# One tile and one transfer for both forms of v, and a new static order, in a one-core attention and mixture-of-experts kernel

## The chip, the core and the metric

The program runs on one core of a Trainium2 chip. The metric is the device time of one execution in microseconds (us). The core's engines work side by side, each through its own fixed list of instructions: TensorE (PE; PEld is its weight load), VectorE (DVE), ScalarE (ACT), GpSimd (POOL) and SyncE (SP), which here only issues transfers (DMAs). An instruction waits only for what it depends on and for what stands ahead of it on its engine.

## What is computed

Three stages over 4 batches of 8 heads, 576 tokens and 64 columns a head, all in float32:

```python
# attention: pooled form plus local form
v_d = v.reshape(B, H, 144, 4, D).mean(axis=3)              # q_d, k_d in the same way
out_up = np.repeat(sm_attn(q_d, k_d, v_d), 4, axis=2)      # 144 pooled queries, 144 pooled keys
mask = np.abs(pos[:, None] - pos[None, :]) < 4             # local: the 7 keys around a query
attn_out = out_up + softmax(where(mask, q @ k.T / 8, -1e9)) @ v
# gate stage on x: 2304 x 512
h = x @ w_in                                               # 2304 x 2048
g = (a0 + a1*h + a2*h**2 + a3*h**3) / (1 + |b0|*|h| + |b1|*h**2 + 1e-6)
x = g @ w_out
# soft routing to 8 experts of 4 slots each, two matrix products per expert, and back to the tokens
logits = x @ phi;  out = softmax_rows(logits) @ experts(softmax_columns(logits).T @ x)
```

## The kernel before

**Attention.** Two heads make a pair; there are 16 pairs, four to a batch. A pair lives in one set of four SBUF tiles (class `Set`, all tiles are called `at`). The first four pairs, 0 to 3, use four different sets, all others use set A. A pair needs `qk` (one transfer, `load_qk`) and v in two forms (`load_v`): `vd` for the pooled form, 80 rows by 1024 floats, and `vw`, 128 rows by 1280 floats, the local windows. For v these are two transfers, 320 and 640 KB. `pool_v` adds the four tokens of a group, in place, with two instructions (72x512 and 72x256). The pooled scores go through `scores_d` (PE `scd`), a maximum and a softmax; `turn_d` turns the 144 pooled keys in two halves of 72 onto partitions (PE `tpd`), `copy_d` copies each half out of PSUM on ACT (72x288), and `av_d` multiplies (PE `avd`, L650) before the local products `av` (L643). Sums go into `x`, which is split in a high and a low part, XH and XL.

**Weights.** Each of 8 blocks of `w_in` and `w_out` arrives as 1 MB of 8-byte words, and DVE narrows it to float32 in three steps (`nar`, `wst`, `wo`; L756, L761, L765). W is split in a high part (a cast) and a low part (a subtraction).

**Gate stage.** One step is 512 tokens by 256 columns: 24 products (PE `hps`, L889, 128x512), then a chain over ACT, DVE and POOL (`activate`: ab, cr, v, a, t, p, ln, ex, e, n, g), then transposes (`gt`), copies and logits (`lg`). Two PSUM pairs take turns: step m uses pair m % 2, and step m + 2 cannot write it until step m's chain has read it for the last time (its `e` or `n`, L990 and L993). The step with number 2, the third, is the first that waits for a pair in this way. The first two steps need all four first pairs of heads; pairs 0, 1, 3, 2 reach `avd` in that order.

**Order.** Nothing is scheduled on the chip. Class `Plan` collects all operations; the table `PLACE` gives each its place in one global order, the table `F` the engine where there is a choice (a ACT, d DVE, p POOL). Each engine gets its instructions in that order. The planner's durations (`PARTS`) and its `simulated` decide two more things: which DMA is held back until an earlier one has landed, and where `fillers` (products on zeros, `lg<-zero`, L1159 and L1162) stand in PE's list, at places where the planner foresees an idle PE.

**End.** The 32 transfers of expert weights (`we`, 1 MB each) run from 322 us on, most of them after 385 us.

Of the kernel before, what the change touches and what calls it, by code (L numbers as in the profile page):

```python
# [24 lines left out]
VROWS = 128  # L25
# [6 lines left out]
    pq="dppppppppdpppppp",  # L32
    pk="pddppppppppppppp",
    pv="pppppppppdpdpppp",
    nl="ppppppppddddppdp",
    nd="pppppppppdppdppd",
    wih="aaaaaaad",
    wil="pppppppd",
    xh="aaaaaaaadadadadda",
    xl="ppppdpdddpppddddd",  # L40
    cr="spppspppppppssppaappdpppppssspappsppa",
    t="dpdpddddddddddddddddpdddddddddddddddd",
    sd="rsssssrrssrsssrs",
    v="pppppppppppppppppdppdppppppppppppdppp",
    a="aaaaaadaaadaaaaaaaaaaaaaadaaaddaaadaa",
    g="ddfdfffddddddddddddddffddddddddddddff",
    gc="aaaaaaaaaadddaaaaadaaaaadadadadaaaaaadadadaadaaaaaaaaaadaadaaaadaaaaadaa",
# [3 lines left out]
    dm=(8,),  # L51
    ldqk=(4, 7, 31, 5, 125, 252, 361, 452, 546, 592, 716, 795, 822, 941, 1027, 1069),
    ldc=(6, 0),
    ldv=(42, 76, 163, 72, 219, 413, 466, 551, 602, 722, 800, 862, 944, 1063, 1092, 1176),
    coef=(1,),
    roots=(2,),
    rooted=(3,),
    pq=(9, 25, 58, 22, 149, 285, 412, 465, 580, 638, 726, 806, 842, 942, 1031, 1117),
    pk=(10, 21, 81, 16, 174, 335, 383, 453, 554, 617, 748, 796, 858, 960, 1033, 1134),
    sc=(17, 24, 44, 27, 236, 331, 437, 510, 585, 634, 744, 816, 895, 972, 1040, 1116),  # L60
    mx0=(18, 29, 52, 38, 250, 347, 440, 521, 590, 657, 746, 821, 901, 977, 1051, 1122),
    ms0=(19, 35, 53, 40, 265, 353, 446, 523, 593, 658, 756, 824, 910, 983, 1054, 1132),
    ex0=(23, 39, 56, 49, 266, 356, 463, 524, 594, 659, 757, 832, 911, 984, 1055, 1133),
    nl=(36, 43, 64, 71, 283, 394, 473, 536, 603, 685, 758, 841, 920, 996, 1067, 1142),
    nlp=(41, 69, 115, 103, 290, 404, 494, 549, 627, 717, 762, 843, 925, 1005, 1068, 1156),
    scd=(11, 55, 97, 26, 226, 336, 432, 504, 586, 695, 772, 812, 888, 981, 1077, 1141),
    mxd=(12, 61, 111, 30, 243, 341, 433, 506, 601, 704, 773, 815, 894, 982, 1085, 1145),
    msd=(13, 70, 116, 33, 263, 350, 451, 512, 616, 706, 777, 819, 897, 986, 1087, 1146),
    exd=(14, 78, 119, 37, 267, 352, 454, 515, 623, 707, 782, 829, 898, 993, 1091, 1152),
    nd=(28, 92, 124, 51, 273, 360, 461, 526, 674, 711, 783, 833, 915, 1035, 1109, 1155),  # L70
    ndp=(45, 99, 137, 84, 274, 391, 475, 535, 687, 725, 787, 840, 922, 1036, 1118, 1157),
    pv=(48, 126, 180, 87, 329, 430, 517, 567, 684, 754, 828, 878, 947, 1073, 1128, 1177),
    tp0=(54, 138, 144, 148, 295, 428, 501, 568, 633, 735, 793, 859, 937, 1022, 1113, 1169),
    cp0=(59, 140, 146, 156, 298, 431, 502, 574, 639, 753, 805, 873, 940, 1041, 1119, 1172),
    tp1=(67, 82, 166, 123, 325, 416, 505, 550, 631, 727, 814, 869, 969, 1023, 1094, 1161),
    cp1=(68, 83, 168, 129, 328, 417, 508, 555, 632, 728, 817, 876, 973, 1039, 1112, 1162),
    td0=(65, 127, 158, 104, 280, 398, 487, 558, 691, 740, 790, 853, 964, 1065, 1124, 1165),
    cd0=(66, 139, 159, 106, 293, 401, 491, 564, 698, 741, 802, 856, 976, 1078, 1125, 1170),
    td1=(47, 130, 142, 107, 275, 392, 482, 556, 690, 765, 811, 861, 935, 1076, 1126, 1163),
    cd1=(50, 136, 143, 108, 287, 393, 488, 561, 697, 766, 813, 867, 939, 1080, 1130, 1164),  # L80
    avd=(75, 141, 182, 162, 372, 460, 520, 569, 699, 775, 831, 881, 1001, 1081, 1131, 1178),
    av=(79, 151, 185, 170, 377, 464, 528, 578, 701, 776, 835, 883, 1002, 1084, 1138, 1179),
    od=(85, 152, 186, 171, 378, 474, 530, 579, 705, 785, 845, 884, 1015, 1086, 1140, 1181),
    x20=(86, 153, 195, 175, 390, 479, 539, 582, 719, 791, 854, 886, 1019, 1100, 1144, 1186),
    x21=(94, 155, 194, 172, 386, 478, 537, 583, 708, 794, 850, 885, 1016, 1099, 1143, 1184),
    x8=(91, 157, 193, 181, 384, 483, 531, 584, 720, 792, 851, 889, 1021, 1102, 1154, 1193),
    xh=(100, 173, 199, 176, 457, 516, 540, 589, 721, 799, 865, 887, 1057, 1108, 1150, 1187, 1300),
    xl=(101, 188, 208, 190, 472, 534, 577, 591, 739, 838, 871, 907, 1088, 1136, 1151, 1188, 1305),
    ldi=(15, 57, 93, 117, 145, 192, 169, 201),
    w0=(32, 60, 77, 110, 132, 135, 160, 167, 203, 196, 206, 183, 211, 209, 268, 278, 309, 311, 359, 355, 406, 408,  # L90
        448, 462, 541, 544),
    w1=(34, 62, 90, 112, 133, 150, 161, 178, 204, 198, 207, 187, 217, 227, 269, 279, 313, 318, 362, 357, 407, 409,
        449, 469, 542, 547),
    w2=(46, 63, 109, 118, 134, 165, 164, 179, 205, 200, 214, 191, 225, 230, 276, 281, 314, 319, 363, 369, 414, 420,
        455, 470, 545, 548),
# [1486 lines left out]
```

## Time and profile before

| | us |
|---|---|
| three runs | 489.97, 492.66, 494.0 (median 492.66) |
| the profiled execution | 491.29 |
| its span, from the first to the last instruction | 489.4 |
| PE busy | 458.5 (94%) |
| DVE busy | 401.6 (82%) |
| ACT busy | 321.1 (66%) |
| POOL busy | 246.8 (50%) |

Busy shares are means over stages. The opening (0 to 70 us) loads and narrows all gate weights and runs the first four pairs; the middle (70 to 380 us) is the gate stage with the other pairs between its steps; the rest are the last block, routing and experts. "Idle before" in a row is how long the engine stood still ahead of the instruction, and what ended that.

### The profile page before, as it was taken

How to read it: one execution, taken by the hardware profiler on the slowest of the kernel's cores; microseconds unless marked ns; L12 is line 12 of the kernel's file. 1: busy time of each engine (PE TensorE's matmuls, PEld its weight loads, DVE VectorE, ACT ScalarE, POOL GpSimd, SP SyncE). 2: the span in 40 equal slices, each digit the busy share in tenths (PEclk: the TensorE clock that was granted, in tenths of full speed). 3: DMA queues.
4: the chain of work that ended last, by engine and by line, in shares of the span. 5: the costliest groups of instructions: out<-in, count | busy, mean ns of one | idle time of the engine just before them, and what ended most of it. 6: DMA issues, size and time to landing. Idle time of an engine off the chain costs nothing.

```text
span 489.4 us, 12949 instructions
## 1 busy us (share of the span) xinstructions
PE 458.5 (94%) x5417; PEld 334.3 (68%) x5417; DVE 401.6 (82%) x568; ACT 321.1 (66%) x682; POOL 246.8 (50%) x231
## 2 busy tenths in 40 slices
PE   8687989999999999999999999999999989799995
PEld 5455766787687778766777676777766886343574
DVE  5799999999899899958898799899899988825233
ACT  3765586988767778866879776666867676610222
POOL 6588777864964557477174656624241514101000
PEclk9889999999999999999999999999999999999997
DMA  8999734566645102312402312380000399999966
GB/s 327 321 362 365 248 117 148 178 211 206 194 121 175 50 27 70 117 55 78 130 1 77 105 60 68 131 321 17 0 1 0 122 389 356 395 425 427 426 258 259
DMA packets 17866, 89.81 MB, mean 184 GB/s; under 512 B 2064, under 2 KB 2576, under 8 KB 11152
## 3 DMA queue, kind: packets, MB, share of 16 engines
q1 hardware_dynamic: 17808, 88.98, 50.4%
q8 instruction: 43, 0.70, 0.6%
q14 instruction: 15, 0.12, 0.1%
HBM read 80.06 MB, written 8.91 MB: 182 GB/s over the span
## 4 chain that ended last, share of the span: by engine, by line
PE 44%; DVE 20%; POOL 13%; ACT 11%; DMA 6%; issue 4%; SPq 0%; DVEq 0%; POOLq 0%; ACTq 0%
PE hps L889 16%; POOL gate L971 7%; DMA at<-in_qk 4%; PE op L1451 3%; DVE gate L990 3%; PE gt L1018 3%; ACT hps L989 3%; PE hps L907 2%; POOL gate L967 2%; DMA wst<-in_w_in 2%; PE av L643 2%; ACT gate L988 2%; PE hp L1330 2%; PE tpd L632 2%; PE scd L590 2%
## 5 line engine op out<-in xcount | busy, mean ns | idle before, releaser
L889 PE MATMUL hps<-XH,W 128*128 128x512 f32 x512 | 169.3, 400 | 1.6 <-DVE wst L765 1.0
L889 PEld LDWEIGHTS hps<-XH,W 128*128 128x128 f32 x512 | 96.6, 189 | 27.9 <-issue 2.5
L971 POOL TENSOR_TENSOR gate<-gate 128x1024 f32<-128x1024 f32 (+1 forms) x34 | 81.1, 2385 | 47.2 <-ACT gate L965 21.9
L889 PE MATMUL hps<-XL,W 128*128 128x512 f32 x256 | 100.4, 392 | 0.0
L967 POOL TENSOR_SCALAR gate<-gate,cf_sb 128x1024 f32<-128x1024 f32 (+1 forms) x25 | 32.1, 1284 | 72.3 <-ACT gate L975 70.1
L988 ACT ACTIVATE gate<-gate,one 128x1024 f32<-128x1024 f32 (+1 forms) x37 | 42.0, 1135 | 33.1 <-POOL gate L971 32.1
L990 DVE SCALAR_TENSOR_TENSOR gate<-gate,hps 128x1024 f32<-128x1024 f32 (+1 forms) x37 | 44.0, 1189 | 13.6 <-ACT hps L989 13.0
L889 PEld LDWEIGHTS hps<-XL,W 128*128 128x128 f32 x256 | 48.4, 189 | 9.1 <-POOL XL L734 0.2
L989 ACT ACTIVATE hps<-gate 128x1024 f32<-128x1024 f32 (+1 forms) x37 | 37.2, 1006 | 8.9 <-DVE gate L987 4.1
L729 ACT COPY G<-gt 128x512 f32<-128x512 f32 x56 | 32.6, 590 | 9.7 <-PE gt L1018 9.4
L564 POOL TENSOR_TENSOR at<-at 128x144 f32<-128x144 f32 x56 | 35.1, 627 | 4.4
L975 ACT ACTIVATE gate<-hps 128x1024 f32<-128x1024 f32 (+1 forms) x29 | 29.0, 999 | 5.4 <-PE hps L889 4.2
L971 DVE TENSOR_TENSOR gate<-gate,hps 128x1024 f32<-128x1024 f32 x24 | 29.2, 1216 | 3.9 <-ACT gate L965 3.8
L1018 PE MATMUL gt<-cf_sb,gate 128*128 128x128 f32 x192 | 28.7, 278 | 2.5 <-ACT G L729 1.1
L1018 PEld LDWEIGHTS gt<-cf_sb,gate 128*128 128x128 f32 x192 | 21.7, 141 | 11.3 <-ACT G L729 3.9
L602 ACT ACTIVATE at<-sc,at 128x38 f32<-128x38 f32 x144 | 28.2, 316 | 0.6
L987 DVE SCALAR_TENSOR_TENSOR gate<-gate,cf_sb,hps 128x1024 f32<-128x1024 f32 x22 | 28.1, 1277 | 0.6
L617 POOL TENSOR_TENSOR at<-at 128x432 f32<-128x432 f32 (+1 forms) x24 | 20.2, 849 | 12.6 <-DVE at L613 9.3
L994 DVE SCALAR_TENSOR_TENSOR gate<-gate 128x1024 f32<-128x1024 f32 x20 | 26.0, 1301 | 0.4
L907 PE MATMUL hps<-xs,W 128*128 128x256 f32 x192 | 24.3, 285 | 1.3 <-DVE A L993 1.2
L965 ACT ACTIVATE gate<-hps,cf_sb 128x1024 f32<-128x1024 f32 x19 | 22.9, 1208 | 3.9 <-PE gt L1018 2.6
L993 DVE SCALAR_TENSOR_TENSOR gate<-gate,cf_sb,hps 128x1024 f32<-128x1024 f32 x20 | 25.5, 1273 | 0.0
(182 smaller groups left out, 981.8 us busy)
## 6 DMA issues: line engine op xcount, KB each, us to landing
we<-in_w SPq DMA_DIRECT2D x32, 1024.0 KB, 10.1
at<-in_vw SPq DMA_DIRECT2D x16, 640.0 KB, 6.0
at<-in_qk SPq DMA_DIRECT2D x16, 579.0 KB, 5.5
wst<-in_w_in SPq DMA_DIRECT2D x8, 1024.0 KB, 8.7
wst<-in_w_out SPq DMA_DIRECT2D x8, 1024.0 KB, 6.0
at<-in_vd SPq DMA_DIRECT2D x16, 320.0 KB, 6.3
out<-late SPq DMA_DIRECT2D x17, 256.0 KB, 2.4
wo_dram<-wo SPq DMA_DIRECT2D x8, 512.0 KB, 7.9
```

The source lines that it names most:

```text
L564: nc.gpsimd.tensor_tensor(out=dst, in0=dst, in1=x[:, :, j], op=ALU.add)
L602: nc.scalar.activation(out=dst[:, i, :], in_=st["s", j][:, i, :], func=ACTF.Exp, scale=scale, bias=mx[:, i:i + 1], accum_out=None if sums ...
L729: nc.scalar.copy(out=out, in_=x)
L889: nc.tensor.matmul(hps[m][:, c].rearrange("p u t -> p (u t)"), lhsT=W[p][:, w, kk, 128 * c:128 * c + 128], rhs=x[xx][:, kk, :], start=(kk ...
L907: nc.tensor.matmul(out[:, c, :], lhsT=W[p][:, w, kk, 128 * c:128 * c + 128], rhs=xs[i][:, xx, kk, :], start=(kk == 0 and j == 0), stop=(kk ...
L967: (nc.vector if who == "d" else nc.gpsimd).tensor_scalar(out=out, in0=x, scalar1=coef[:, w:w + 1], scalar2=coef[:, b:b + 1], op0=ALU.mult, ...
L971: turned_over((nc.vector if who == "d" else nc.gpsimd).tensor_tensor(out=out, in0=x, in1=y, op=op), who)
L975: do("ab", "B", "H", lambda B, H: act(out=B, in_=H, func=ACTF.Abs, scale=coef[:, 4:5] if s2 else 1.0))
L988: do("ln", "C", "B", lambda C, B: act(out=C, in_=B, func=ACTF.Ln, bias=one))
L989: do("ex", "H", "C", lambda H, C: act(out=H, in_=C, func=ACTF.Exp, scale=-1.0))
L990: do("e", "B", "H", lambda B, H: stt(out=B, in0=B, scalar=1.0 + 1e-6, in1=H, op0=ALU.add, op1=ALU.mult))
L1018: nc.tensor.transpose(gt[n][:, u, 128 * c:128 * c + 128], g_of(n, c)[:, 128 * u:128 * u + 128], idn)
```

## The change

**Layout.** `v` is one array of 128 rows by 1792 floats: 1280 for the windows as before, and two areas of 256 for pooled keys 0 to 111 of either head (112 rows). Keys 112 to 143 of both heads lie in the last 256 of the window's columns, on rows 64 to 127, which the windows leave unused. One transfer of 896 KB takes the place of 320 and 640 KB, so 64 KB fewer for each pair, and 16 transfers fewer. Tiles are cut anew: V alone in the fourth tile, the turned scores and the gate's spare buffer in the second.

**Pooling v.** Three instructions take the place of two: 128x384, 128x128, 64x64. `pool_v` no longer overwrites v, but the next transfer of v waits for both the pooling and `av`; before, `vd` waited for the pooling and `vw` for `av`.

**Products.** Keys are turned as 112 and 32. Copying the 32 takes two ACT copies of 32x144 (one to each head's partitions), the 112 one of 112x288. `av_d` still has four products. Areas that must be zero are set once at the start by 8 more POOL memsets.

**Order and engines.** `PLACE` is new throughout, and `F` partly: the high part of the last W block goes from DVE to ACT. The planner's loads and fetch waits are costed differently. PE's list has 33 wide and 22 narrow fillers where it had 25 and 7; in each, six or seven wide ones open the program, and 6 wide ones stand in the last third.

```diff
-            self.qk, pdt, vds = cut(tags[0], 2 * S + 2 * PAD, 576, 256)
+            self.qk, pdr, half = cut(tags[0], 2 * S + 2 * PAD, 288, 384)
...
-            self.Vd, self.spare = cut(tags[3], 1024, 1024)
+            self.V, vds = cut(tags[3], 1792, 192)
...
     def load_v(s, bb, p):
-        begin(out=s.Vdl, in_=vd[bb, p])
-        begin(out=s.V[0:VROWS], in_=vw[bb, p])
+        begin(out=s.V, in_=v[bb, p])
...
-            turned_over(eng.tensor_tensor(out=x, in0=x, in1=y, op=ALU.add), who)
-            eng.tensor_tensor(out=dst, in0=x[:, 0:256], in1=x[:, 256:512], op=ALU.add)
+            turned_over(eng.tensor_tensor(out=s.half, in0=s.Vd[:, :, 0:128], in1=s.Vd[:, :, 128:256], op=ALU.add), who)
+            for r, b in ((slice(0, 128), slice(1, 3)), (slice(64, 128), slice(0, 1))):
+                eng.tensor_tensor(out=s.VdS[r, b], in0=s.half[r, b, 0:64], in1=s.half[r, b, 64:128], op=ALU.add)
...
+            for h in range(2):
+                x = st["t", 4][0:32, 64 * h:64 * h + 1]
+                nc.scalar.copy(out=s.PdR[64 + 32 * h:96 + 32 * h, h].rearrange("p (i q) -> p i q", i=3),
+                               in_=bass.AP(tensor=x.tensor, offset=x.offset, ap=[list(x.ap[0]), [136, 3], [1, 48]]))
...
+                nc.tensor.matmul(o, lhsT=s.VdS[0:LONG, 1 + h, :], rhs=s.PdT[0:LONG, h, :], start=True, stop=False)
+                nc.tensor.matmul(o, lhsT=s.VdS[:, 0, :], rhs=s.PdR[:, h, :], start=False, stop=True)
...
-        do("pv", "pv", pool_v, who["pv"], w="v VdS", pick=("pv", index))
+        do("pv", "pv", pool_v, who["pv"], r="v", w="VdS", pick=("pv", index))
...
-    wih="aaaaaaad",
+    wih="aaaaaaaa",
...
-    ldqk=(4, 7, 31, 5, 125, 252, 361, 452, 546, 592, 716, 795, 822, 941, 1027, 1069),
-    ldv=(42, 76, 163, 72, 219, 413, 466, 551, 602, 722, 800, 862, 944, 1063, 1092, 1176),
+    ldqk=(0, 11, 47, 6, 96, 275, 362, 452, 543, 575, 672, 795, 839, 919, 991, 1063),
+    ldv=(40, 58, 134, 80, 205, 408, 492, 547, 673, 716, 810, 867, 958, 1049, 1082, 1152),
```

On SP, the start of the program. Before (`at` is a set's tile, `wst` a raw weight block, `cf_sb` and `cb_sb` constants):

```order
L427 DMA cf_sb<-in_cf 128x390
L427 DMA at<-in_qk 128x1158 x2
L427 DMA cb_sb<-in_cb 128x470
L427 DMA at<-in_qk 128x1158
L427 DMA wst<-in_w_in 128x2048
L427 DMA wst<-in_w_out 128x2048
L427 DMA at<-in_qk 128x1158
L427 DMA at<-in_vd 80x1024
L427 DMA at<-in_vw 128x1280
```

Of the change:

```order
L421 DMA at<-in_qk 128x1158
L421 DMA cf_sb<-in_cf 128x390
L421 DMA at<-in_qk 128x1158
L421 DMA cb_sb<-in_cb 128x470
L421 DMA wst<-in_w_in 128x2048
L421 DMA at<-in_qk 128x1158
L421 DMA wst<-in_w_out 128x2048
L421 DMA at<-in_v 128x1792
```

The first weight block moved ahead of the third `qk`, and the fourth `qk` out of this stretch (it stands two transfers further on).

On DVE, the first weight blocks among the first pairs. Before (`at<-scd` and `at<-sc` are maxima of pooled and local scores; the second row of maxima here is that of pair 1's pooled scores):

```order
L595 TENSOR_REDUCE at<-sc 128x9
L756 TENSOR_SCALAR nar<-wst 128x1024
L595 TENSOR_REDUCE at<-scd 128x3
L761 SCALAR_TENSOR_TENSOR nar<-wst,nar 128x1024
L765 SCALAR_TENSOR_TENSOR wo<-wst,nar 128x1024
```

Of the change (L670 are pair 0's three sums after `av`):

```order
L759 TENSOR_SCALAR nar<-wst 128x1024
L589 TENSOR_REDUCE at<-sc 128x9
L606 TENSOR_REDUCE at<-at 128x9
L607 RECIPROCAL at<-at 128x9
L764 SCALAR_TENSOR_TENSOR nar<-wst,nar 128x1024
L768 SCALAR_TENSOR_TENSOR wo<-wst,nar 128x1024
L759 TENSOR_SCALAR nar<-wst 128x1024
L670 TENSOR_TENSOR at<-avd,at 128x4x64
L670 TENSOR_TENSOR at<-av,at 128x4x64
L670 TENSOR_TENSOR X_85<-av,at 128x64
L589 TENSOR_REDUCE at<-scd 128x3
```

The maximum of pair 1's pooled scores moved behind the whole `w_out` block and pair 0's sums.

On PE, what stands between the 24 products of a gate step and pair 7's pooled product `avd`, with the last of the 24 as the first row (`av` of the pair before stands right ahead of the 24, in both). Before:

```order
L889 MATMUL hps<-XH,W_983 128x512
L623 MATMUL tp<-cf_sb,at 38x128
L1018 MATMUL gt<-cf_sb,A_1087 128x128 x4
L632 MATMUL tpd<-cf_sb,at 72x128 x3
L842 MATMUL wq<-cf_sb,pp 128x32 x2
L632 MATMUL tpd<-cf_sb,at 72x128 x3
L823 MATMUL wt<-cf_sb,wo 128x128 x8
L623 MATMUL tp<-cf_sb,at 102x128 x4
L650 MATMUL avd<-at 64x144 x4
```

Of the change:

```order
L892 MATMUL hps<-XH,W_999 128x512
L617 MATMUL tp<-cf_sb,at 38x128
L627 MATMUL tpd<-cf_sb,at 112x128 x3
L629 MATMUL tpd<-cf_sb,at 32x128 x3
L845 MATMUL wq<-cf_sb,pp 128x32 x2
L617 MATMUL tp<-cf_sb,at 102x128 x4
L826 MATMUL wt<-cf_sb,wo 128x128 x4
L653 MATMUL avd<-at 64x144
```

Four transposes `gt` and four `wt` moved out of the stretch between the two products.

## Rows read from the trace of the kernel before

**Rows 1.** By stretch: length, then busy us (instructions) per engine, PEclk, DMA share, GB/s

```profile
0.00:12.50 12.50, 10.16 (x191) 6.93 (x194) 6.94 (x24) 4.69 (x17) 7.87 (x28) 1.00 0.86 328
12.50:20.00 7.50, 4.28 (x152) 3.37 (x152) 7.03 (x13) 5.06 (x27) 3.32 (x5) 0.78 1.02 346
...
22.40:70.60 48.20, 41.46 (x567) 29.59 (x567) 45.94 (x69) 30.44 (x62) 38.44 (x31) 0.93 0.77 266
70.60:380.00 309.40, 303.26 (x3456) 227.81 (x3455) 278.17 (x355) 234.38 (x489) 176.30 (x154) 1.00 0.32 104
380.00:440.00 60.00, 54.06 (x450) 38.87 (x450) 44.51 (x55) 33.94 (x58) 16.76 (x11) 1.00 0.87 341
440.00:489.40 49.40, 43.31 (x606) 26.59 (x598) 18.94 (x58) 10.36 (x20) 1.85 (x1) 0.95 0.84 343
```

**Rows 2.** Chain that ended last, 30 to 75 us: start, length, what

```profile
34.04 9.99 DMA wst<-in_w_in
...
44.12 0.71 DVE nar L756
...
69.43 1.19 DVE gate L993
```

**Rows 3.** Timeline of DVE and PE, 17 to 71 us: start, length, what, idle before

```profile
18.41 0.52 DVE L595 TENSOR_REDUCE at<-sc 128x9 f32<-128x342 f32 x1 [0.33 <-PE sc L580]
...
22.37 0.61 DVE L595 TENSOR_REDUCE at<-scd 128x3 f32<-128x432 f32 x1 [2.31 <-PE scd L590]
...
27.71 0.74 DVE L560 TENSOR_REDUCE at<-at 128x144 f32<-128x576 f32 x1
...
66.28 0.71 DVE L731 CAST W<-wst 128x1024 fp32r<-128x1024 f32 x1
...
69.34 1.27 DVE L993 SCALAR_TENSOR_TENSOR gate<-gate,cf_sb,hps 128x1024 f32<-128x1024 f32 x1
...
66.68 2.42 PE L1159 MATMUL lg<-zero 128*96 128x256 f32 x10
...
70.67 0.50 PE L889 MATMUL hps<-XH,W 128*128 128x512 f32 x1
```

**Rows 4.** Packets, rate, share of 16 engines: 42:44, 444:446 and 302.5:308 us

```profile
DMA packets 108, 0.47 MB, mean 235 GB/s; under 512 B 12, under 2 KB 12, under 8 KB 105
...
q1 hardware_dynamic: 108, 0.47, 103.4%
...
DMA packets 114, 0.84 MB, mean 422 GB/s; under 512 B 11, under 2 KB 11, under 8 KB 11
...
DMA packets 241, 1.00 MB, mean 182 GB/s; under 512 B 32, under 2 KB 32, under 8 KB 240
...
q1 hardware_dynamic: 240, 0.98, 54.1%
```

**Rows 5.** One steady hand-over: window transfer of v, landing, next product

```profile
136.08 0.33 SPq L427 DMA_DIRECT2D at<-in_vw  x1
...
at<-in_vw SPq DMA_DIRECT2D x1, 640.0 KB, 5.4
...
143.41 1.07 PE L823 MATMUL wt<-cf_sb,wo 128*128 128x128 f32 x8
...
144.84 0.72 PE L650 MATMUL avd<-at 72*64 72x144 f32 x8
145.49 0.66 PE L1018 MATMUL gt<-cf_sb,A 128*128 128x128 f32 x4
```

**Rows 6.** Groups by line and shape: busy us, mean ns, idle before

```profile
L570 POOL TENSOR_TENSOR at<-at 72x512 f32<-72x512 f32 x14 | 18.0, 1283 | 7.0 <-DMA at<-in_vd 3.2 <-DVE gate L971 2.1 <-DVE at L617 1.7
...
L636 ACT COPY at<-tpd 72x288 f32<-72x288 f32 x32 | 12.5, 398 | 7.7 <-PE tpd L632 7.0
...
L571 POOL TENSOR_TENSOR at<-at 72x256 f32<-72x256 f32 x14 | 10.2, 728 | 1.1
...
L654 ACT ACTIVATE at<-avd 128x144 f32<-128x144 f32 x16 | 4.8, 301 | 8.4 <-PE avd L643 8.3
```

More of the change, by code (lines that the diff above doesn't have):

```diff
@@ L66 @@
[L66 to L71, printed above, removed]
@@ new lines @@
+    wor=(1354,),
+    h8=(1363, 1370, 1361, 1364, 1387, 1388, 1391, 1393, 1411, 1415, 1413, 1414, 1443, 1444, 1450, 1451),
+    we=(1158, 1291, 1409, 1383, 1368, 1474, 1510, 1462, 1500, 1402, 1394, 1421, 1416, 1503, 1518, 1452, 1537, 1533,
+        1519, 1494, 1516, 1532, 1540, 1534, 1535, 1560, 1554, 1577, 1546, 1548, 1593, 1574),
+    zm=(1428,),
+    gst=(1528,),
+    inv=(1538,),
+    gt0=(1529,),
+    gt1=(1530,),
+    sl=(1531,),
+    si0=(1541,),
+    si1=(1539,),
+    si=(1542,),
+    z=(1543,),
@@ new lines @@
+    l1=(1544, 1545, 1547, 1549, 1550, 1555, 1557, 1559),
+    z2m=(1572,),
+    hs0=(1561,),
+    hs1=(1568,),
+    ht=(1570,),
+    z2=(1573,),
+    c1=(1551,),
+    c2=(1552,),
+    c3=(1553,),
+    cs=(1556, 1565, 1562, 1558, 1575),
+    ct=(1569, 1576, 1563, 1566, 1588),
+    cc=(1571, 1578, 1564, 1567, 1589),
+    l2=(1579, 1580, 1581, 1582, 1583, 1584, 1585, 1586, 1590, 1595, 1602, 1604, 1608, 1613, 1614, 1617, 1592, 1594,
+        1623, 1627, 1634, 1640, 1643, 1644),
+    os=(1587, 1618, 1647),
@@ L194 @@
+    s4=(1591, 1626, 1648),
+    s4h=(1596, 1630, 1649),
+    s4l=(1597, 1635, 1655),
+    o=(1598, 1600, 1610, 1603, 1619, 1620, 1606, 1611, 1628, 1637, 1636, 1645, 1651, 1656, 1663, 1672, 1669, 1666,
+        1659),
+    out=(1607, 1622, 1629, 1615, 1641, 1631, 1625, 1632, 1653, 1646, 1642, 1654, 1657, 1660, 1665, 1674, 1671, 1668,
+        1662),
 )
@@ L281, in fetch @@
     def fetch(self, now):
-        queued = next((x for t, x in reversed(self.known) if t <= now), 0.0)
-        return max(1.0, queued - now) + 2.5
+        return 7.5 if now < 60 else 5.0 if now < 400 else 6.5
     def fetched(self, start, us, calls):
@@ L288, in fetched @@
             return us
[L289 removed]
+        for k in range(max(-2, (self.ran - FIRST) // BLOCK), (self.ran + calls - FIRST) // BLOCK + 1):
             for x in (FIRST + BLOCK * k, FIRST + BLOCK * (k + 1) - AHEAD):
@@ L314, in order @@
     def order(self, banks):
-        self.sent = []
-        for _ in range(3):
-            self.known = self.sent
-            done = self.simulated(banks)
-        return done
+        return self.simulated(banks)
     def simulated(self, banks):
@@ L405, in attn_moe_moe_kernel @@
 @with_exitstack
-def attn_moe_moe_kernel(ctx, tc, qk, vw, vd, w_in, w_out, w1, w2, cf, cb, out):
+def attn_moe_moe_kernel(ctx, tc, qk, v, w_in, w_out, w1, w2, cf, cb, out):
     nc = tc.nc
@@ L1534 @@
     win = win.reshape(B, H // 2, 64, 5, 2, 4 * D).transpose(0, 1, 4, 2, 3, 5)
+    vs = np.zeros((B, H // 2, 128, 1792), np.float32)
+    vs[..., 0:1280] = win.reshape(B, H // 2, 128, 1280)
+    vd = v.reshape(B, H // 2, 2, 144, 4 * D)
+    for h in range(2):
+        vs[:, :, 0:LONG, 1280 + 256 * h:1536 + 256 * h] = vd[:, :, h, 0:LONG]
+        vs[:, :, 64 + 32 * h:96 + 32 * h, 1024:1280] = vd[:, :, h, LONG:144]
     arrays = {
```

306 lines of the change are left out of this document (137 added, 169 removed), and 14 rows, old and new, of tables (gc, tr).

## The prediction, made blind

> **What bounds the kernel now.** I read the stretches first, since the page's shares are means over very different stages. In [rows 1] the reader sees PE standing still for 309.40 - 303.26 = 6.1 us in the whole middle, and about as much in the two last stretches (60.00 - 54.06 = 5.9 and 49.40 - 43.31 = 6.1). PE is the bound from 70.6 us on: an engine elsewhere gives or takes time there only where it makes PE wait, or where PE's own list changes. PE's useful products are the same in both kernels, so behind 70.6 us there is little to win.
>
> The opening is different. PE is idle for 48.20 - 41.46 = 6.7 us between 22.4 and 70.6 us [rows 1], and part of what it does there is filler: 2.42 us in ten records, five wide products, end just ahead of the third gate step [rows 3]. DVE is full: 45.94 of 48.20 us [rows 1]. The timeline shows the link: L993 on DVE runs from 69.34 for 1.27 us, to 70.61, and the third gate step's first product starts on PE at 70.67 [rows 3]. The chain of waits passes the same way: a `w_in` transfer, DVE's `nar`, DVE's L993 [rows 2]. So **the third step starts when DVE has worked off its list**, and all that PE does behind it moves with it. Where DVE stood still before: 12.50 - 6.94 = 5.56 us up to the first weight block, 0.47 in the next stretch [rows 1], 2.31 waiting for pair 1's `scd` [rows 3], and 48.20 - 45.94 = 2.26 in the rest [rows 1]: 10.6 us together. That sum and DVE's work are what the opening can give.
>
> **The change, part by part.**
>
> *DVE's work ahead of L993.* The order shows four differences: one cast of W less (0.71), one pooling reduction of q or k less (0.74), one maximum of pooled scores less (0.61), one of local scores more (0.52) [rows 3]. That is -1.5 us. What left DVE stands now on ACT and POOL, which have 48.20 - 30.44 = 17.8 and 48.20 - 38.44 = 9.8 us idle there [rows 1]; if they turn out late, the 1.5 us are lost again.
>
> *The first weight block.* One `qk` fewer stands ahead of `w_in`: 128 x 1158 floats are 0.593 MB, at the first stretch's 328 GB/s [rows 1] 1.8 us. DVE's 5.56 idle us can shrink by that, if the transfer is all it waits for. But pair 1's scores come later by the same. Bounds 0 and -1.8; I take -1.2.
>
> *The maximum of pair 1.* DVE's 2.31 us wait [rows 3] goes, since that instruction now stands behind a whole `w_out` block. What is late next is that block's own transfer. Bounds 0 and -2.3; I take -1.5.
>
> *One transfer for v.* Before, 80 + 128 rows, now 128. In a crowded 2 us (share 103%) 108 packets were under way or served, nearly all between 4 and 8 KB [rows 4]: 2 x 1.03 x 16 / 108 = 0.31 us of one DMA engine for a packet. Where mostly v moves, 240 packets took 54.1% of 16 engines for 5.5 us [rows 4]: 0.20 us each. So 208 packets cost 2.6 to 4.0 us of all 16 engines. For 128 packets of 7 KB the nearest row is 8 KB packets: 0.84 MB in 2 us at 422 GB/s [rows 4], by which 0.917 MB cost 2.2 us. Saved: 0.4 to 1.8 us of the queue for a pair, 1.7 to 7 for the first four. Of this only what DVE waits for counts, at most the 2.26 us; bounds 0 and -2.3, and I take -0.8.
>
> The Trainium skill, DMA: Bandwidth & Descriptors, section Specifications, gives 512 B as the smallest transfer for full rate; by it rows of 4 and 5 KB are as good as rows of 7 KB. Then merging saves only the 64 KB, 0.15 us for a pair at 422 GB/s [rows 4], so the term would be about -0.2 (0.6 us for four pairs, of which the same small part counts) instead of -0.8, and the sum 0.4 us higher. The trace does not bear that out so far: 235 GB/s at a full share against 422 [rows 4], with rows of different lengths.
>
> These four terms make -1.5 - 1.2 - 1.5 - 0.8 = -5.0, with bounds 0 and -7.9. They don't simply add: an engine that runs earlier soon stands before data that is not there. I take 0.7 of it, **-3.5 us**.
>
> *Fillers.* By the order 12 wide ones, in runs of 3 and 9, stand before the third step where 8 stood. One costs 2.42 / 5 = 0.48 us [rows 3], four 1.9. They lie in PE's 6.7 idle us [rows 1]: 0. If the third step is ready before they are through, +1.9.
>
> *Pooling on POOL.* Before, 1.283 + 0.728 = 2.01 us [rows 6]. The two shapes give (1283 - 728) / 256 = 2.17 ns a column and 0.17 us fixed, so 384, 128 and 64 columns cost 1.00 + 0.45 + 0.31 = 1.76 us, a quarter of a us less; POOL has 309.40 - 176.30 = 133 us idle [rows 1]: 0. The 8 memsets at the start meet a POOL that is idle for 12.50 - 7.87 = 4.6 us [rows 1]: 0, at worst the fixed 0.17 us each, +1.4.
>
> *Copies of turned keys on ACT.* Two copies of 72x288 (0.398 each) become one of that size and two of 32x144, for which 128x144 with 0.301 is the nearest [rows 6]: 2 x 0.301 - 0.398 = +0.2 us for a pair, +3.3 for 16. ACT has 309.40 - 234.38 = 75 us idle in the middle [rows 1], so 0; if every one lay on PE's path, +3.3.
>
> *The hand-over of v in the middle.* This is the part that adds a wait. One transfer now waits for the later of pooling and `av`, and the next pair's `avd` waits for transfer and pooling in turn. Before, `vd` was free early, as soon as it was pooled, and only `vw` waited for `av`. In [rows 5] `vw` is issued at 136.08 when `av` is through, and `avd` starts at 144.84: a gap of 8.76 us, filled with 24 gate products, turns and others. Of the change, this place lost four `gt` and four `wt` (0.66 and half of 1.07 [rows 5]; 1.1 to 1.2 us), so the gap is about 7.6 us. What must fit in: 0.33 for the issue, the landing, 1.76 for pooling. With a landing of 5.4 as the 640 KB had in company [rows 5] this makes 7.5, and PE does not wait. With another 256 KB at 328 GB/s [rows 1] it is 8.3: PE waits 0.7 us, and behind `avd` stand `gt` and the next gate step, for which ACT and DVE wait in turn. With a landing of 2.2 us at the rate of 8 KB packets it is 4.3. Eleven pairs follow one another in set A; about five of their gaps in the new order are as short as this one. Bounds 0 and 11 x 0.7 = +7.7; I take **+1.0**, nearer to the row with the landing of 5.4, since 54% of the DMA time at such a place [rows 4] leaves room.
>
> **Sum.** The profiled execution took 491.3 us (span 489.4), which is 1.4 below the median 492.66 of runs from 489.97 to 494.0. 491.3 - 3.5 + 1.0 = **488.8 us**.
>
> **The rivals.**
> - *The opening gives nothing.* What left DVE makes ACT or POOL the last in the chain, and L993 starts when it did. For it: POOL's 38.44 of 48.20 us [rows 1]; against it, ACT's 17.8 us idle. Then 491.3 + 0 to 1.9 (fillers), less at most 0.8: 490.5 to 493.2.
> - *The opening gives all.* DVE loses its 1.5 us of work and its waits down to the rest, and no hand-over makes PE wait: 491.3 - 7.9 = 483.4, up to 486.5. For it: nothing but DVE's list ends at 70.61 [rows 3]; against it, that a later `qk` delays pair 1.
> - *The hand-over decides, and the kernel is slower.* If the landing takes 7.6 us (5.4 x 896/640 [rows 5]), the need is 9.7 against a gap of 7.6: 2.1 us at each short gap. With five of them +10.5, with the opening's -3.5 this is 498.3; with 0.7 at each of eleven 495.5. It turns slower than before from about 0.3 us at each of eleven, that is from a landing of some 5.8 us if all gaps were like this one. For it: `vw` alone has taken 5.4 us; against it: before, the two forms' packets lay in each other's way, and 7 KB rows are nearer to those at 422 GB/s [rows 4].
>
> **How the numbers follow.** Chances: the forecast with 486.5 to 491 as its own range 0.42; opening gives nothing 0.17; opening gives all 0.19; hand-over decides 0.22 (494 to 500). A measurement of this kernel can tell about 1% (4.9 us) from no change, so faster means below 487.7 and slower above 497.6. Of the forecast 0.18 lies below 487.7, and all of the 0.19: faster 0.37. Of the hand-over's 0.22, 0.14 lies above 497.6: slower 0.14. Within 1%: 0.24 + 0.17 + 0.08 = 0.49. The range is 484 to 497.5: it leaves out the slow end (0.14) and the last tail of the second rival (0.03).
>
> **What would show it.** Right: the third step's first product at about 67 us instead of 70.67; DVE's idle time before it at 7 us instead of 10.6, with the first `nar` near 11 us and no 2 us wait for pair 1's `scd`; a v transfer of 128 packets that take less of the engines' time than 208 did; PE's idle time in the middle near 7 us. The hand-over's step is wrong if PE waits for POOL or for `in_v` ahead of `avd` more than a few us in all, or if POOL's pooling never waits for the transfer. The opening's step is wrong if the third step starts on time and an ACT or POOL instruction ends right ahead of it, or if it starts earlier and the 3.5 us come back as PE's idle time behind it, for instance in the last 110 us, where the transfers of expert weights hold 0.84 to 0.87 of the DMA time [rows 1]: then PE is not the bound there, and the whole premise falls.

## The result and the profile after

The changed kernel takes 497.80 us (median of 10 runs, 494.99 to 500.9) against 493.06 us of 10 runs of the kernel before: ratio 1.0114, 95% interval 1.0081 to 1.0146. It is 1.1% slower, where 0.8% faster was forecast. The profiled execution took 497.91 us, span 495.9, which is close to its median; the one of before took 491.29, span 489.4, which is 1.8 below its median. So 6.5 us are to be found in the two traces, where the medians lie 4.7 apart.

By stretch, with the columns and nearly the edges of [rows 1]:

```profile
0.00:12.50 12.50, 11.45 (x192) 7.98 (x192) 7.76 (x23) 4.57 (x19) 7.77 (x33) 1.00 0.87 339
12.50:22.40 9.90, 6.96 (x173) 4.97 (x161) 8.38 (x14) 8.21 (x36) 7.29 (x13) 0.75 1.01 416
22.40:68.20 45.80, 42.78 (x606) 32.31 (x602) 41.88 (x66) 33.20 (x78) 39.09 (x37) 0.94 0.60 235
68.20:380.00 311.80, 301.44 (x3423) 226.01 (x3422) 274.40 (x349) 237.29 (x482) 159.03 (x153) 0.99 0.31 107
380.00:440.00 60.00, 56.03 (x443) 40.43 (x446) 46.10 (x54) 38.16 (x64) 21.47 (x13) 1.00 0.64 245
440.00:495.90 55.90, 47.77 (x641) 28.77 (x633) 20.45 (x60) 10.90 (x21) 1.85 (x1) 0.96 0.94 387
```

In the middle PE is idle 311.80 - 301.44 = 10.4 us instead of 6.1, and its granted clock is no longer 1.00 throughout. In the last 116 us the load on the DMA engines has moved to the end: 0.64 and 0.94 where [rows 1] has 0.87 and 0.84.

The opening, from the timeline of DVE and PE (start, length, what, idle before), as in [rows 3]:

```profile
10.18 1.22 DVE L759 TENSOR_SCALAR nar<-wst 128x1024 int32<-128x1024 int32 x1
...
22.99 0.42 DVE L670 TENSOR_TENSOR at<-avd,at 128x256 f32<-128x256 f32 x1 [1.90 <-ACT at L657]
...
24.55 0.61 DVE L589 TENSOR_REDUCE at<-scd 128x3 f32<-128x432 f32 x1 [0.68 <-PE scd L584]
...
66.71 1.27 DVE L996 SCALAR_TENSOR_TENSOR gate<-gate,cf_sb,hps 128x1024 f32<-128x1024 f32 x1
...
62.01 4.16 PE L1162 MATMUL lg<-zero 128*96 128x256 f32 x18
...
68.23 0.50 PE L892 MATMUL hps<-XH,W 128*128 128x512 f32 x1
```

The third step starts at 68.23 us instead of 70.67: 2.4 us earlier. From there to the end it takes 495.9 - 68.2 = 427.7 us, where before it took 489.4 - 70.7 = 418.7. **The opening won 2.4 us and what follows lost 9.0.**

### The profile page after: what moved, and what is told of

The parts are those of the page before. It is cut to its first block, busy times and chain, and to the rows that moved or that the text cites. A ratio compares the mean times of both kernels' runs of the same rounds, so it can differ in the third digit from the quotient of the medians.

```text
span 495.9 us, 13015 instructions
## 1 busy us (share of the span) xinstructions
PE 466.4 (94%) x5448; PEld 340.5 (69%) x5448; DVE 399.0 (80%) x564; ACT 332.3 (67%) x696; POOL 236.5 (48%) x246
## 4 chain that ended last, share of the span: by engine, by line
PE 43%; DVE 21%; ACT 12%; POOL 10%; DMA 9%; issue 4%; SPq 0%; DVEq 0%; POOLq 0%; ACTq 0%
PE hps L892 19%; DMA we<-in_w 7%; POOL gate L974 6%; PE gt L1021 3%; DVE gate L993 3%; ACT hps L992 2%; PE av L646 2%; ACT gate L991 2%; DVE gate L974 2%; POOL gate L970 2%; ACT gate L978 2%; PE dsp L1093 2%; DVE nar L759 2%; DVE nar L764 2%; DMA wo_dram<-wo 2%
## 5 line engine op out<-in xcount | busy, mean ns | idle before, releaser
L974 POOL TENSOR_TENSOR gate<-gate 128x1024 f32<-128x1024 f32 (+1 forms) x32 | 77.9, 2435 | 50.6 <-ACT gate L979 12.0
L970 POOL TENSOR_SCALAR gate<-gate,cf_sb 128x1024 f32<-128x1024 f32 (+1 forms) x21 | 25.1, 1195 | 52.9 <-ACT gate L978 49.7
L611 POOL TENSOR_TENSOR at<-at 128x342 f32<-128x342 f32 (+1 forms) x29 | 24.1, 834 | 35.2 <-DVE at L607 15.1
L732 ACT COPY G<-gt 128x512 f32<-128x512 f32 x55 | 31.6, 583 | 8.5 <-PE gt L1021 8.3
L974 DVE TENSOR_TENSOR gate<-gate,hps 128x1024 f32<-128x1024 f32 x24 | 29.1, 1211 | 5.7 <-ACT gate L968 5.6
L559 POOL TENSOR_TENSOR at<-at 128x144 f32<-128x144 f32 x50 | 31.1, 622 | 3.9
L997 DVE SCALAR_TENSOR_TENSOR gate<-gate 128x1024 f32<-128x1024 f32 x20 | 29.2, 1460 | 0.3
L968 ACT ACTIVATE gate<-hps,cf_sb 128x1024 f32<-128x1024 f32 x22 | 26.5, 1210 | 2.9 <-PE gt L1021 2.8
L996 DVE SCALAR_TENSOR_TENSOR gate<-gate,cf_sb,hps 128x1024 f32<-128x1024 f32 x20 | 25.5, 1274 | 0.0
```

What stands on the lines that cost most here:

```text
L559: nc.gpsimd.tensor_tensor(out=dst, in0=dst, in1=x[:, :, j], op=ALU.add)
L732: nc.scalar.copy(out=out, in_=x)
L970: (nc.vector if who == "d" else nc.gpsimd).tensor_scalar(out=out, in0=x, scalar1=coef[:, w:w + 1], scalar2=coef[:, b:b + 1], op0=ALU.mult, ...
L974: turned_over((nc.vector if who == "d" else nc.gpsimd).tensor_tensor(out=out, in0=x, in1=y, op=op), who)
L997: do("g", "A", "B" + n, lambda A, B, n: turned_over(stt(out=A, in0=B, scalar=-2.0, in1=n, op0=ALU.add, op1=ALU.mult), "d"), pick=("g", m))
```

## Where the 9 us went

**First stall, PE ahead of `avd` of pair 4, 2.1 us.** The timeline of several engines:

```profile
93.76 0.69 DVE L759 TENSOR_SCALAR nar<-wst 128x512 int32<-128x512 int32 x1 [1.57 <-DMA wst<-in_w_out]
...
96.53 0.69 DVE L768 SCALAR_TENSOR_TENSOR wo<-wst,nar 128x512 int32<-128x512 int32 x1 [1.35 <-DMA wo_dram<-wo]
97.14 1.21 DVE L974 TENSOR_TENSOR gate<-gate,hps 128x1024 f32<-128x1024 f32 x1
...
99.72 0.69 DVE L768 SCALAR_TENSOR_TENSOR wo<-wst,nar 128x512 int32<-128x512 int32 x1
...
98.38 1.03 ACT L992 ACTIVATE hps<-gate 128x1024 f32<-128x1024 f32 x1 [2.15 <-DVE gate L974]
...
100.55 0.47 PE L653 MATMUL avd<-at 112*64 112x144 f32 x4 [2.12 <-DVE wo L768]
```

DVE waits first for block 4 of `w_out` and then until block 3's `wo` is stored; both stand in its list ahead of L974, a link of the gate chain, which starts about 3 us late, and ACT behind it. Why should `avd` wait for `wo`? It reads nothing of it. In the built program the scratch `nar` of the block's second half and this `avd` lie in the same PSUM bank. The bank is free only when the last step of that narrowing (L768 at 99.72) has read it; the two waits make that step late, and PE stands before the bank. The transfers were issued at 87.69 and 88.07; the view of DMA issues (KB each, us to landing) has

```profile
wst<-in_w_out SPq DMA_DIRECT2D x1, 1024.0 KB, 6.0
...
wo_dram<-wo SPq DMA_DIRECT2D x1, 512.0 KB, 8.4
...
at<-in_v SPq DMA_DIRECT2D x1, 896.0 KB, 7.7
```

**Second stall, PE ahead of `scd` of pair 6, 2.0 us.** The third of these landings is v of pair 5, which goes into set A behind pair 4:

```profile
103.49 0.33 SPq L421 DMA_DIRECT2D at<-in_v  x1
...
111.22 1.02 POOL L563 TENSOR_TENSOR at<-at 128x384 f32<-128x384 f32 x1 [2.81 <-DMA at<-in_v]
...
113.26 0.57 POOL L557 TENSOR_TENSOR at<-at 128x144 f32<-128x144 f32 x1
...
115.64 2.23 POOL L559 TENSOR_TENSOR at<-at 128x144 f32<-128x144 f32 x2
...
117.92 0.95 PE L584 MATMUL scd<-at 64*64 64x144 f32 x12 [2.04 <-POOL at L559]
```

POOL waits 2.81 us for v; behind it in its list stands the pooling of q and k of pair 6, which needs nothing of that v, and `scd` waits for that.

**The clock.** In windows (length, PE busy, granted clock, DMA share, GB/s), two around the first stall and one later:

```profile
98.00:102.50 4.50, 2.38 (x64) 1.00 0.28 29
102.50:106.50 4.00, 4.00 (x47) 0.57 0.94 340
273.00:277.00 4.00, 4.00 (x11) 0.57 0.64 219
```

PE stood still for nearly half of the first window; then, busy without a gap, it runs at the lower level, 1.2 instead of 2.4 GHz, for 3.4 us, which costs 1.7. The same happens once more at 273 us. The trace of before has no such fall between 70.6 and 380 us (clock 1.00 in [rows 1]).

That is one execution of each kernel. Over 106 runs of the kernel before, taken beside the experiments, the mean granted clock of a run (1.00 is the upper level throughout) lies between 0.963 and 0.991, on average at 0.980; over the 10 of the changed kernel it lies between 0.978 and 0.992, on average at 0.982. So the falls set these two executions apart, and not the two kernels as they were timed.

**The end.** The list of waits of PE from 440 us on begins with

```profile
PE op L1454 <- DMA we<-in_w: 2.3, 2, 2.0
```

(total, times, longest). Before, no wait for `we` of that size is there; of its 32 transfers the new order issues 13 after 440 us, the old one 7. A part of the 2.3 us is won back behind it. The first product on these weights starts, before and after, at

```profile
439.52 13.94 PE L1330 MATMUL hp<-we,Z 128*32 128x512 f32 x128 [0.25 <-issue]
```

```profile
444.69 13.94 PE L1333 MATMUL hp<-we,Z 128*32 128x512 f32 x128 [0.25 <-issue]
```

and from there to the end it takes 489.4 - 439.5 = 49.9 and 495.9 - 444.7 = 51.2 us: the end loses 1.3.

Together 2.1 + 2.0 + 2 x 1.7 + 1.3 = 8.8 us; two waits of before, of 1.1 and 0.9 us, are gone, which leaves 6.8 of the 9.0. For the rest there are waits of PE of 0.5 to 1.0 us, most of them on DVE's gate chain; they are not added up here.

## The experiments

Two theories: **O**, the new order loses the time; **L**, the layout with its single transfer loses it. The tables and the planner of either kernel can be run on the code of the other. Order means `PLACE` and `F` together; no run takes these two apart. All ratios are to the kernel before.

| run | layout | order | ratio | 95% interval |
|---|---|---|---|---|
| changed kernel | new | new | 1.0114 | 1.0081 to 1.0146 |
| a_order | old | new | 1.0098 | 1.0068 to 1.0129 |
| b_layout | new | old | 0.9927 | 0.9898 to 0.9955 |
| b_again | new | old | 0.9935 | 0.9906 to 0.9964 |
| c_swap | new | new, one exchange on DVE | 1.0058 | 1.0033 to 1.0083 |
| d_stall2 | new | new, one exchange on POOL | 1.0067 | 1.0029 to 1.0105 |
| e_both | new | new, both exchanges | 1.0014 | 0.9975 to 1.0053 |
| c_fill | new | new, products on zeros in the stall | 1.0078 | 1.0044 to 1.0111 |
| h1_open | new | new to step 2, then old | 0.9970 | 0.9938 to 1.0002 |
| h1_again | new | the same | 0.9944 | 0.9914 to 0.9973 |
| h2_rest | new | old to step 2, then new | 1.0155 | 1.0104 to 1.0205 |
| h3_late | new | old to step 6, then new | 1.0033 | 1.0005 to 1.0061 |
| h4_early | new | new to step 6, then old | 1.0059 | 1.0036 to 1.0082 |
| g_split | new, v in two transfers | old | 0.9969 | 0.9934 to 1.0004 |

### Order or layout

The edit of a_order, in before's code (b_layout is the same the other way round):

```diff
-    wih="aaaaaaad",
+    wih="aaaaaaaa",
...
-    ldv=(42, 76, 163, 72, 219, 413, 466, 551, 602, 722, 800, 862, 944, 1063, 1092, 1176),
+    ldv=(40, 58, 134, 80, 205, 408, 492, 547, 673, 716, 810, 867, 958, 1049, 1082, 1152),
...
-        queued = next((x for t, x in reversed(self.known) if t <= now), 0.0)
-        return max(1.0, queued - now) + 2.5
+        return 7.5 if now < 60 else 5.0 if now < 400 else 6.5
```

> The layout, the two v transfers and the pooling of before, with the whole new order: PLACE, F, the planner's costs, and so the 33 wide and 22 narrow fillers. Theory O (the order loses the time): after the third step's start, which comes near 68 us as in the changed kernel, PE stalls about 2 us near 100 us, because avd waits for a PSUM bank that DVE's narrowing of w_out holds while DVE waits for DMAs; ratio to before 1.006 to 1.012. Theory L (the layout with its one transfer loses it): the opening's 2.4 us remain and nothing is lost behind it, ratio 0.993 to 0.998.

> The new layout, the one v transfer and the new pooling, with the whole order of before (PLACE, F, planner, 25 wide and 7 narrow fillers). Theory O: 0.997 to 1.003, third step near 70.5 us, no PE stall over 1.3 us in the middle. Theory L: 1.008 or more, PE waiting behind the pooling of v or in_v at several hand-overs.

Measured: 1.0098 and 0.9927. Theory L falls: the layout alone is 0.7% faster, faster than both kernels. The order alone is 1.0% slower, and has the same first stall with two v transfers. From its timeline:

```profile
102.97 0.72 PE L644 MATMUL avd<-at 72*64 72x144 f32 x8 [2.12 <-DVE wo L759]
...
119.56 0.95 PE L584 MATMUL scd<-at 64*64 64x144 f32 x12 [1.39 <-POOL at L558]
```

In b_layout the third step starts at 69.15 us, in a_order at 70.56, where before has 70.67: on the old layout the order wins 0.1 us of the opening. The layout's 1.5 us can't be read as its own, since the mean granted clock up to the third step is 0.95 in b_layout and 0.93 in a_order and before. On the new layout the new opening does start the third step earlier: at 66.40 to 68.55 us in eight profiled executions, with 68.66 to 69.61 in five with the old opening. From the third step to the end b_layout takes 488.1 - 69.15 = 419.0 us, as long as before (418.7). And PE's list of waits in b_layout from 68 to 396 us begins

```profile
PE avd L652 <- issue: 1.0, 1, 1.0
PE wt L832 <- ACT at L646: 0.8, 1, 0.8
PE scd L590 <- DVE X L676: 0.7, 1, 0.7
```

so with the old order no product waits for v or its pooling that I could call a cost of the hand-over.

### The two stalls, taken away

c_swap lets L974 of step 3 pass the first half of block 4's narrowing on DVE, and so gives `avd` another bank:

```diff
-    w0=(..., 312, 317, 352, 364, 410, ...
+    w0=(..., 312, 317, 363.2, 366.2, 410, ...
```

(w1 and w2 in the same way; the planner's fillers are left as they were.)

> The changed kernel with one exchange on DVE alone: the gate chain's L974 product of step 3 stands ahead of the first half of w_out block 4's narrowing instead of behind it; every other engine's list is the same. Theory O: L974 starts near 94 us instead of 97.1, narrowing ends 1 us earlier, PE's 2.12 us stall ahead of avd near 100 us shrinks to 1.0 us or less, and if the clock then does not fall to half at 102.7 us for 3.4 us, that is worth another 1.7 us: ratio to before 1.003 to 1.009 where the changed kernel has 1.011. If the stall comes from something else (ACT's copies, or PE's own instruction supply) it stays and the ratio is 1.010 to 1.012.

d_stall2 lets the pooling of q and k of pair 6 pass the pooling of v of pair 5 on POOL:

```diff
-    pq=(1, 36, 94, 15, 238, 315, 429, ...
+    pq=(1, 36, 94, 15, 238, 315, 408.4, ...
```

> The changed kernel with one exchange on POOL alone: the pooling of q and k of pair 6 stands ahead of the pooling of v of pair 5 instead of behind it. Theory O with the hand-over of v on POOL: PE's 2.04 us stall ahead of scd near 116 us goes, ratio to before 1.006 to 1.008. Rival: the wait only moves, since the gate chain behind it on POOL or avd is late next: 1.010 to 1.012.

Measured 1.0058 and 1.0067, both as theory O had it. In c_swap's timeline

```profile
92.20 1.22 DVE L974 TENSOR_TENSOR gate<-gate,hps 128x1024 f32<-128x1024 f32 x1 [1.79 <-POOL gate L974]
...
96.82 0.47 PE L653 MATMUL avd<-at 112*64 112x144 f32 x4 [0.33 <-ACT G L732]
```

0.33 us are left of the 2.12 (this execution is 1.8 us ahead from the opening on), and the clock does not fall behind it. In d_stall2 `scd` follows the products ahead of it without a gap:

```profile
116.25 0.85 PE L574 MATMUL sc<-at 64*32 64x38 f32 x72
117.03 0.96 PE L584 MATMUL scd<-at 64*64 64x144 f32 x12
```

Its profiled execution was one of its longest (498.0 us span, three stretches at the lower clock level in the middle, 17 us together), so what it shows beyond that is not read here.

> The changed kernel with both exchanges, on DVE (L974 of step 3 ahead of the first half of w_out block 4) and on POOL (pooling of q and k of pair 6 ahead of the pooling of v of pair 5). Alone they gave 1.006 and 1.007 where the changed kernel has 1.011. If the two stalls add: 1.000 to 1.003. If POOL's exchange only moves its wait to tp and tpd of pair 6, as its profile suggests: 1.004 to 1.007. The order's loss of 1.9% against the layout alone (1.011 against 0.993) is then to be sought in smaller waits of the middle.

Measured 1.0014: the two add. They are 1.0 of the 1.8 points between the new and the old order under the new layout (1.0114 against 0.993).

### Stall or clock

c_fill leaves the stall's cause and puts products on zeros into it:

```diff
+            elif self.items[n][0] == 378:
+                self.idle(0, 4)
```

> The changed kernel with four wide products on zeros (about 1.8 us) ahead of the avd of pair 4, in the place of the 2.12 us stall near 100 us; the stall's cause stays. If PE's idle time is what lets the clock fall to half at 102.5 us, the fall goes and 1.7 us are won: 1.007 to 1.009. If the clock falls for another reason, or the products come on top: 1.011 to 1.014.

Measured 1.0078. The first two windows lie over the same times as above:

```profile
98.00:102.50 4.50, 4.50 (x93) 1.00 0.80 213
102.50:106.50 4.00, 4.00 (x30) 1.00 0.93 382
271.00:275.00 4.00, 4.00 (x13) 0.57 0.56 215
319.00:323.00 4.00, 4.00 (x43) 0.57 0.01 4
```

This execution is 1.8 us ahead at the stall (`avd` at 98.78 us). The products cost nothing, as PE would have waited, and the clock stays at 1.00 there. But this execution falls to the lower level twice later on, as often in all as that of the changed kernel, and its span is 496.7 us against 495.9. The two ratios' intervals overlap (1.0081 to 1.0146 and 1.0044 to 1.0111). So the fall behind this stall goes when the stall is filled; that the kernel as a whole gains 1.7 us by it is not shown.

The other traces agree for this place. Four have the stall of 2.0 to 2.1 us unfilled (the changed kernel, a_order, d_stall2, h4_early), and in each the clock falls right behind it, for 3.4 us in two and about 6.8 in two; in c_swap, e_both and c_fill, where it is gone or filled, there is no fall. Yet a long stall is not enough, and a fall needs none: the second stall, of 1.4 to 3.2 us in five traces (the changed kernel, a_order, c_swap, c_fill, h2_rest), has no fall behind it, and the fall at 273 us follows waits of 0.36 and 0.51 us. What decides it stays open.

### Which part of the order

The order was cut at the third step's first product, and at the seventh's. The operations that one order has ahead of the cut are put in the sequence of the other; the rest keep theirs, in `PLACE` and in `F` (all on the new layout, with the changed kernel's planner). One line of h1_open against the changed kernel, the places of the pooling of q by pair, new up to pair 4 and old from pair 5 on:

```diff
-    pq=(1, 36, 94, 15, 238, 315, 429, 459, ...
+    pq=(1, 36, 94, 15, 238, 285, 412, 465, ...
```

> The new layout; the new order up to the third step's first product (260 operations), from there the order of before; planner and 33 wide fillers of the new one. Known so far: old order all through 0.993, new order all through 1.011. Theory M (the new order's middle loses the time by itself, its opening wins): 0.987 to 0.991, third step near 68 us. Theory C (the third step that starts earlier collides with the w_out transfers, which come no earlier; the gain is given back whatever the order behind it): 0.992 to 0.996, with a DVE wait on in_w_out or wo_dram and a PE stall between 90 and 120 us.

> The new layout; the order of before up to the third step's first product (256 operations), from there the new order; the new planner. Theory M: the stalls near 100 and 116 us are there, all comes 1 to 2 us later than in the changed kernel, 1.010 to 1.016. Theory C: with the later third step the waits of DVE on w_out shrink, ratio 0.998 to 1.006.

Measured 0.9970 and 1.0155. h2_rest is as M had it, and not as C had it: with a later opening the new rest is no better, so the rest loses by itself. But h1_open is in neither range: M's opening wins nothing. Repeated beside the layout alone:

> The new layout with the whole order of before, once more, beside the next two on one chip. It gave 0.993 (0.990 to 0.996). Expected 0.990 to 0.996.

> The new layout, the new order up to the third step's first product and the old one behind it, once more. It gave 0.997 (0.994 to 1.000), though its profiled execution is 1.2 us shorter than that of the layout alone. If the new opening wins: 0.988 to 0.992, below the layout alone; if it gives nothing or loses in most executions: 0.993 to 0.999.

0.9935 and 0.9944: the opening of the new order is worth nothing that can be measured, though its third step started at 66.88 and 68.55 us in two executions, with 69.15 and 69.61 for the old one. The timeline of h1_open has waits of PE that neither execution of the old opening has:

```profile
74.45 0.50 PE L599 MATMUL tpd<-cf_sb,at 128*32 128x128 f32 x3 [1.30 <-POOL at L581]
...
122.40 0.63 PE L991 MATMUL gt<-cf_sb,gate 128*128 128x128 f32 x4 [1.52 <-DVE wo L738]
```

In it DVE waits 1.75 us for `in_w_out` (up to 71.62) and 1.50 for the store of `wo` (up to 117.61). In h1_again all four waits are there too, with 1.25, 0.54, 1.66 and 0.51 us. The two waits of DVE are what C foresaw for the opening, an earlier third step that meets transfers which come no earlier, and 0.9944 lies in C's range; that these waits take the whole gain was not shown. That the planner and its fillers, which are new here, cost little is shown by the same run.

Ahead of the new rest, the timeline of h2_rest has the stalls too, the second one longer:

```profile
88.21 0.66 PE L991 MATMUL gt<-cf_sb,gate 128*128 128x128 f32 x4 [1.38 <-DVE wo L738]
...
101.73 0.47 PE L623 MATMUL avd<-at 112*64 112x144 f32 x4 [0.86 <-DVE wo L738]
...
118.89 0.95 PE L554 MATMUL scd<-at 64*64 64x144 f32 x12 [3.20 <-POOL at L529]
```

> The new layout; the old order up to the seventh gate step's first product (step 6, near 126 us), the new order behind it. It leaves out the opening of the new order and both stalls near 100 and 116 us. Known: old all through 0.993, new all through 1.011, old opening with all the rest new 1.016, the two stalls taken away by exchanges 1.001. If the two stalls are the new order's whole loss: 0.991 to 0.996. If a second half of it lies in many small waits behind 126 us: 0.999 to 1.004.

> The new layout; the new order up to the seventh gate step's first product, the old order behind it: the complement. If the stretch up to 126 us holds the whole loss: 1.008 to 1.013. If half of it: 1.001 to 1.005. Added to the run of the old order up to there, the two differences to 0.993 should make about 1.011 - 0.993 = 0.018.

Measured 1.0033 and 1.0059; to 0.993 that is 1.0 and 1.3 points, together 2.3 where 1.8 was to be made (each interval is 0.5 wide). So the loss lies on both sides of 126 us. Ahead of it are the stalls: the trace of h4_early has the first (2.12 us, with 6.8 us at the lower clock level behind it), but only 0.24 us of the second. Behind it are waits, of which the list of h3_late from 126 us on begins with

```profile
PE op L1424 <- DMA we<-in_w: 1.7, 2, 1.0
PE hps L862 <- DVE gate L966: 1.0, 1, 1.0
PE avd L624 <- POOL at L535: 1.0, 1, 1.0
```

The third stands near the seam of the two orders and is that hybrid's own; so are 0.7 us more just ahead of it and 6.8 us at the lower clock level behind it, in the longest execution of the twelve (498.26, median 494.28). The others are the changed kernel's too. That these are the whole late loss was not shown by taking them away.

### One transfer or two

```diff
-        begin(out=s.V, in_=v[bb, p])
+        begin(out=s.V[:, 1024:1792], in_=v[bb, p][:, 1024:1792])
+        begin(out=s.V[:, 0:1024], in_=v[bb, p][:, 0:1024])
```

> The layout alone (order of before) with the transfer of v split in two again: columns 1024 to 1791 (384 KB, 128 rows of 3 KB) first, columns 0 to 1023 (512 KB, rows of 4 KB) behind it: 256 packets where the one transfer has 128, the same bytes. If it is the fewer packets that make the layout 0.7% faster (the prediction's term for v): 0.997 to 1.002, with the first weight block and the third step later by 1 to 2 us. If it is the bytes, the pooling or the products: 0.990 to 0.995.

Measured 0.9969, an interval that holds both expectations. The trace tells more. The pages' third part (packets, MB, share of 16 engines) for before, b_layout and g_split, in this order:

```profile
q1 hardware_dynamic: 17808, 88.98, 50.4%
```

```profile
q1 hardware_dynamic: 16272, 87.93, 48.2%
```

```profile
q1 hardware_dynamic: 18576, 87.93, 48.3%
```

With the spans of 489.4, 488.1 and 488.4 us the engines worked 246.7, 235.3 and 235.9 us. The layout saves 11.4 us of DMA time, 0.7 for a pair, but splitting each transfer again, with 2304 packets more, gives 0.6 of it back: the saving is not the number of packets. The third step starts at 68.66 us in g_split, not later than in b_layout (with a mean granted clock of 0.98 up to there against 0.95). What of the layout makes it faster, its 64 KB less for a pair, the pooling, the products or the places of the tiles, stays open. So does the clock's part in it: the mean granted clock of a run is 0.988 on average over the 24 of b_layout and b_again, and 0.980 over the 106 of before.

## Right and wrong, step by step

- **The opening, -3.5 us.** It was -2.4 in the profiled execution, so the size was not far off, but the cause was. DVE's idle time up to the third step was to fall from 10.6 to about 7 us; it is 4.7 + 1.5 + 3.9 = 10.2. The first `nar` came 2.3 us earlier, even more than taken, and the wait for pair 1's `scd` fell from 2.31 to 0.68; but DVE then waited 1.90 us for pair 0's `od` on ACT and again elsewhere. Taking 0.7 for terms that do not add was too much. What is left is DVE's shorter list; and L996 ends at 67.98, when PE is still at `scd`, with 4.2 us of fillers ahead of that: PE sets the start as much as DVE. So it did before, where one more filler than [rows 3] shows runs up to the third step:

```profile
69.98 0.65 PE L1159 MATMUL lg<-zero 128*96 128x256 f32 x2
```

Timed, the order's part of the opening was nothing; h1_open's trace has waits of 1.30 and 1.52 us behind it.
- **The rank of causes** was turned round: the prediction gave the order's new opening most of the gain and the layout's transfer the only loss. The layout gains 0.7% and the order loses.
- **"PE is the bound from 70.6 us on ... little to win."** PE is busy for 301.4 of 311.8 us of the middle, so the premise holds there, and the step that failed is the one drawn from it: the middle was costed only at the hand-over of v. That PLACE is new throughout was costed at nothing, with the sentence that PE's useful products are the same. The same work in another order costs 1.8% on the new layout (1.0114 against 0.993), 9 us. PE's idle time in the middle is 10.4 us where about 7 was to be the sign of being right. The weight blocks' narrowing ahead of a gate link, the pooling of q and k behind that of v and the 13 late `we` transfers all stand in the lists of order, the PSUM bank follows from them, and none was looked at.
- **The hand-over, +1.0.** The rival's price of a landing (7.6 us, from 5.4 x 896/640) met the first one, 7.7. What was late next was not `avd`, as the prediction named it, but the pooling behind it on POOL and `scd`. That is 2.0 us, once, and it depends on the order; with the old order no such wait shows. The eleven-fold price was wrong: no other hand-over of the changed kernel makes PE wait more than 0.5 us.
- **v's transfer, -0.8.** 0.7 us of DMA time for a pair was within the 0.4 to 1.8. (The row of 42:44 does not show that its packets lie "between 4 and 8 KB": 93 of 108 lie between 2 and 8.) The step behind it, a fixed cost for a packet, fell with g_split. The rule of the Trainium skill, DMA: Bandwidth & Descriptors, section Specifications, that transfers run at full rate from 512 B on, was weighed there and set aside; g_split agrees with it (rows of 3 and 4 KB against 7 KB: 235.9 and 235.3 us). The 0.15 us for a pair that the prediction drew from it, the 64 KB alone, falls short of the 0.7, though; what else is saved no run here shows.
- **Fillers, POOL's pooling, ACT's copies at 0.** In b_layout neither POOL's pooling nor ACT's copies show as a wait of PE but for one: 0.8 us behind ACT's copy L646, at a place where before has 0.55. The new fillers end at 66.4 us in the changed kernel, L996 at 67.98, so they did not hold the third step up.
- **The clock** was no term at all, since it was 1.00 in the middle of before. Two falls cost 3.4 us in the profiled execution; over all runs the two kernels' mean granted clocks are alike (0.980 and 0.982).
- **The rivals.** "The hand-over decides" had the right sign, 0.22 of the chance and 495.5 to 498.3. That 497.80 lies in there is luck: the rival had 7.7 to 10.5 us of waits ahead of `avd`, and of its mechanism there are 2.0 us, once, ahead of `scd`. A rival was missing: that a new order puts an instruction that waits for a DMA ahead of one on PE's path.

## What to carry to other kernels

A new layout and a new static order are two changes; where the tables can be run on the other's code, run them crosswise before anything else. A changed order is to be costed like any other change: list on each engine the instructions that wait for a DMA, and look at what stands right behind each and who shares its buffers, a PSUM bank used as scratch among them. Here the best of all kernels is the new layout with the old order (b_layout and b_again, 0.993).

## What was not expected of the hardware

In each of the four traces that have it, a PE stall of 2.0 to 2.1 us was followed by 3.4 or about 6.8 us at 1.2 GHz, while another, of 1.4 to 3.2 us in five traces, was not; filling the first one with products that nobody needs kept the granted clock at 1.00 there. A transfer of 512 KB to DRAM took 8.4 us to land beside 1 MB that took 6.0, and it was the store that held DVE last.
